# Output projection of the last batch as Strassen blocks, with a new order of all operations

## The chip, the cores and the metric

The kernel runs on one core of a Trainium2 chip. The core has five engines that run side by side and wait for one another through semaphores: TensorE (PE in the profile; its weight loads are PEld), VectorE (DVE), ScalarE (ACT), GpSimd (POOL) and SyncE (SP, which here only issues DMAs). The time is the device time of one execution in microseconds.

## The reference

Attention over 4 batches and 8 heads of 768 tokens, in which k and v are first mixed by an 8 x 8 matrix that five rounds of normalising have made nearly doubly stochastic; then a bilinear feed-forward layer on the result.

```python
def _moe_ref(x, w_a, w_b, w_out):      # x: 3072 x 512, one row for each token
    a = x @ w_a                        # 512 x 1536
    b = x @ w_b
    return (a * b @ w_out).astype(np.float32)   # 1536 x 512
```

The change touches the last product, `(a * b) @ w_out`, for the 768 tokens of the last batch. Below, h stands for `a * b`, and hT for h transposed, as the kernel keeps it.

## The kernel before

Each batch goes through attention (by pairs of heads), through the products with w_a and w_b, and through the product with w_out. Several batches are under way at once: attention of batch b+2 lies between the feed-forward work of batches b and b+1, and the loads run ahead of that.

**Feed-forward, batch 0** (`ab_plain`): four matmuls of 384 columns for each block of 128 features, then on ACT a copy of a and on DVE a product into hT.

**Feed-forward, batches 1 to 3** (`ab_strassen`, PE line L954): a and b by Strassen's method in Winograd's form. Both halves of the tokens and both halves of the features make up a 2 x 2 block problem, which takes 7 block products instead of 8. The features are cut into 6 groups g; in each group PE runs seven products p1 to p7, each a block of four matmuls of 384 columns. Two PSUM pairs take them, kA and kX. ACT copies the running sum of kA to SBUF three times (`snap`, L960: s1, u2, u3); DVE adds kX to these copies (`plus`, f<-f,ps: c11, c22, c12); four products make hT, of which one reads PSUM and runs on DVE (h21, hT<-a,ps, after an ACT cast, L990) and three read SBUF (hT<-f) and run on POOL or DVE. The fifth product of a group waits for c11, the third for c22, since they share kX. The sums of x that these products need are `x_sums` (tx), those of the weights `w_sums` (ws_a, ws_b, 128x768 each).

**Output** (`out_plain`, L1011): for each half t of the tokens and each chunk c of 128 columns, 12 matmuls of 512 columns add up over the 12 feature blocks in one PSUM bank; ten of them may run before the last group of h is done. Then a copy to SBUF on ACT or DVE (L317 and L319) and two stores from SP (L1031).

**The order.** Every piece of work is added to a `Plan` with the engines that may do it. `solve` doesn't choose: it reads the order of all pieces, and the engine of each, from the byte string `ORDER`, two digits of base 91 for each piece (its number times two, plus which of its engines). So ORDER fixes the queue of every engine. Engines take their queues in order; an instruction that waits holds up all that stand behind it on its engine. DMA loads are issued by POOL, and stand in its queue beside its arithmetic.

**Taking turns.** Pieces marked `port=("POOL", "DVE")` (sums with both inputs in SBUF, and hT<-f) must not run on POOL and DVE at the same time: `emit` makes the next one wait for the last one of the other engine.

```python
            if op.eng in op.port:
                for e, name in ported.items():
                    if e != op.eng:
                        tc.add_manual_dep(new[0], name, info, reason="one of them at the port")
                ported[op.eng] = new[-1].name
```

**Which output is used** is chosen near the end of the kernel function. Before, STRASSEN_OUT is empty, so all four batches use `out_plain`:

```python
        if b in STRASSEN_OUT:
            if wt_ok is None:
                wt_ok = o_sums(RB - 10.0)
            out_strassen(b, RB + 40.0, wt_ok)
        else:
            for t in range(2):
                for c in range(3):
                    out_plain(b, t, c, RB + 40.0)
```

Of the kernel before, what the change touches and what calls it, by code (L numbers as in the profile page):

```python
# [36 lines left out]
class Plan:  # L37
# [192 lines left out]

RATE = 365e3
ORDER = (
    b"$e1;%z###%#'#)#+#/#-#1#5$g$i#7#;$k$m#A$o#=$q$s#G#3$u$w#C#M$y%^${#I$}#9#S%`%#%%#Y%'#O#?%)%+"
    b"#`#E%-%/#U#f%1%~%3#[#K%5#l&$%7%9#b#r%;#Q%=#W%?#x%A#h%C&@#~%E#n#^%G&B%I$(%K#t%M#d$.%O%Q%S#j"
    b"$4#z%U&_$$#p%W$*&a%Y%b$0%f#v$:%d%[$6&&%h'&)#&g#|&(&H&j%n$&'A%j&K$,&*%p&2%m$<$2&L)'&,&D&O&4"
    b"&k&G%r&n&P'^%t&.$8&R$@%v&c$B$F&1&e%x&T%}'''z)%&}&V')&X&6$>'#&o&8'Y&:$H&q'`&Z$L']&<'b&s&^'="
    b"&?'h&u'?'C&w$N$D$R'+'j'd'.'v-b'E'g&y'/'x&|'G'|'1'J*($T$J(#$X'3**'5-n'7((*0($*,$Z$P('(**@$_"
    b"(,(6*.(.(0(<$a'9$V*B';*2(B*X*H(H*4-j(8'l$]*6'n'p*](>*<'r(N*Z-V't(D$c-R*L(T*a(:-_*_(Z(J-T*8"
    b"(@(a-Z(P+f-X(g*N(F+i*c(m(V*:(L(s+j-]*T(]+^*>-d(R+l'K,4(c+a*e'M(X,6,,(y(i'O(_,.-h*g'Q(o'S*i"
    b"*m(e'U(u,]'X)),X(k-a(2)/,T({,Z,_*k(q)5(4,W)+,a-));*q*o(w-+,c)A,i*s(},k)G+b-l*y*P*}+d)1,8-f"  # L240
    b"+x)-,;+#+z,e+n*R+p)M,g*D*V)S+r)7*F-p+t+)+%+v)3,0*J+|)Y,2+'+~+9,$)=,<++,F,>)C+;)9)`+-,H)I,@"
    b"+A,J)?)f,B+/,D)O+=)E)l+5,L,N)U--+?-/)K+E)[)r+C-1+I)Q)x)b+G-3)W)~+K+M.R)h)^+O+1.T,m)n)d+3,o"
    b",q,s+Q+7,u)j.Z-5+S)t.],w-7+Y/%,y._+U,{/')p/U)z/Q+W.a/W)v-%+[*u*$-'/S/-*w//)|.c-9,&,(-C*{-;"
    b".*-E/1,}.e*&-=-G/~-?.H-I-A,*-K,P/3.,-#-M/)../Y.V/+/[0$.0.J.X/C.M/9.4/E/5,R/^/;.N-O.q.g.s.6"
    b".21=/p.8.u/7.>.w/r.:1@/`.i.P.k.<.@1A/f/b.m.B-r1C/h.D.o/d.y0*/=.F0,/G-|/?0./I/A00/K/j0&/l1j"
    b"/n0(-t021l06-w0@-~0804-x1r.%0B1n1t.&1E1p-z/t1G1x/v2-1v1z/x.(1M1~0:1O1|0<2$2/2(0>1S2&1I1U2*"
    b"0D201W0F1K221`0H1Q1d241b260N1Y2:0P0T281[2<0Z0V2@1^2>2B0]0a2Q2V0R1i0g2D2F2X0m0X4L2L1g2_0c4N"
    b"2N2H0s0i2S2a4P0y2Z2J0_4H0o2e1#2]0e3C2g4R2c0k3E2u4J2i2k4T2T3K2q4{2s3M1)0u0q2m2x4w1/4}3Q2o0{"
    b"4V155#3S3G2z2{4y5%0w3U2}3I5'5K0}4X3^3'1%3c5M3O3`3)3#3W5)4]3-3%4_3d4Z3Y3/3>4g1+3+1'3[4i5+31"
    b"5G11333f5-59396D5O5;3;353?5Q1-3r17.{.}5I37135S3B0J5x3t5z4a/z3w3h/#4c195t5[3x5|5^5U3|5~0L/M"  # L250
    b"4e/|4k6$3~4m5W5f4o4$5v5/3j5h4&443m513z3n/O53465566576&485=4>5Y5?684:5A4(6I6(3p6N4<5`6F6P5j"
    b"4@5b6*6J4*4B5d4D6L5l5n6R6V4F6T8(6X4,8*6]6n6Z4.806_408,826c6a8.6o86426i6e6k888F846g8:8<6q7`"
    b"8B6,8D7b8H8>7d6.8@7h7f8J6s7j607l8#6u627n646{7p6w6}7t7r7%6y8$7z7v7'7|757#7x6:7)7+8&7;716<7-"
    b"787=737C7/7?7E6>798L7A7I8N8P7Z7K8T8R7M8V8l8X7U8Z7W7G8]8{7O8a7[7Q8n8c7S8q4q6@8e7^4s8p6B8_9G"
    b"5C8g9Q4u8i5p5E8}9I9#8s5r9L9)9%8u9S9M9'9=9V8w9O939W8y9Y9?9[9A9+9^9C9`9.9d9b9/959f:$9E9{979j"
    b":&999h91:(9l:,9p9;9n:.:*9|9r9v:29t:B:0:49x9~:H:8:6:J:L:E:>:P:N:::R:@:g:T:<:V:G;5:X;9;7:]:Z"
    b";;:i;=:c:_;S:e;?;A:a;C:l:m;E:q:o;I;G:s;U:u;O;K;Q:w;/:y;M:{;X;Y:};^;[;%;#;`;1;';+;b;-;x;f;)"
    b";d<,;4;h<@;j;n;{;p;l;r<T;t;};v<B<6<D<F<.<V<0<H;~<Y<2<Z<8<4<$<:<J<'<<<]<(<L<><N<P<*<R"
)
STRASSEN_OUT = ()  # L260
QDMA = lambda b, p: 4 * b + p >= 10
VDMA = lambda b, p: 4 * b + p >= 6
XDMA = lambda p: False
# [4 lines left out]
def kernel(  # L268
# [959 lines left out]
    for b in range(B):  # L1228
        if b in STRASSEN_OUT:
            if wt_ok is None:  # L1230
# [112 lines left out]
```

The softmax here doesn't subtract the row's maximum and nothing guards it: scores larger than these inputs give would overflow.

## Time and profile before

| | us |
|---|---|
| median of 7 runs | 245.35 (244.51 to 245.63) |
| the profiled execution | 244.51 |
| its span, first to last instruction | 242.7 |
| PE busy by stretch: 0 to 20, 20 to 40, 40 to 60 | 16.64, 18.69, 20.00 |
| PE busy 100 to 120, 180 to 200, 230 to 243 | 19.76, 20.00, 8.19 |
| DVE busy 100 to 120, 160 to 180, 180 to 200 | 17.93, 16.06, 8.36 |
| POOL busy 100 to 120, 180 to 200 | 13.09, 2.63 |
| granted TensorE clock, mean | 0.996 of full |

Busy time is read per engine and stretch; a PE that is busy all through may still run below its rate, since the ends of matmuls are modelled and overlap. A group's row names line, engine, operation, what is written and read, shapes, how many, then busy time, mean of one in ns, and the idle time before them with what ended it. In a timeline each row has start, duration, engine, line, operation and count, and in brackets the idle time before it.

The last products with w_a and w_b end at 226.8 us; from there on PE runs only output matmuls of batch 3, until 238.2.

### The profile page before, as it was taken

What the parts mean: (1) busy time and instruction counts of PE and PEld (TensorE: products, weight loads), DVE (VectorE), ACT (ScalarE), POOL (GpSimd) and SP (SyncE); (2) the same over time, 40 slices, a digit from 0 to 9 for tenths busy, and PEclk for the clock granted to TensorE, in tenths of its full rate; (3) what the DMA queues carried; (4) which work ended last, traced back from release to release, by engine and by line L of the source; (5) the groups of instructions that cost most, each with busy time, mean ns of one, the idle gap of its engine ahead of it and who ended that gap; (6) DMA issues with size and microseconds to landing.
All of it is one profiled execution on the core that took longest, in us unless ns stands there. A gap on an engine that the chain in (4) does not pass through costs nothing.

```text
span 242.7 us, 5334 instructions
## 1 busy us (share of the span) xinstructions
PE 232.6 (96%) x2125; PEld 130.7 (54%) x2125; DVE 154.3 (64%) x309; ACT 118.1 (49%) x177; POOL 101.9 (42%) x116
## 2 busy tenths in 40 slices
PE   8699989999999999999999999999999999999992
PEld 3367655656665445565554455556554455555440
DVE  6658748737574616699899346678873248874520
ACT  3268635764455452856664242665612066563110
POOL 8769899996610020039933020254120205433000
PEclk9999999999999999999999999999999999999998
DMA  5999999999997965509999787200008650000066
GB/s 69 170 188 116 201 174 194 201 208 195 193 206 150 132 171 130 120 1 120 141 162 185 148 197 167 58 0 4 0 0 122 140 125 5 3 0 0 0 132 130
DMA packets 54296, 28.27 MB, mean 116 GB/s; under 512 B 33536, under 2 KB 51200, under 8 KB 54272
## 3 DMA queue, kind: packets, MB, share of 16 engines
q0 software_dynamic: 26704, 14.16, 45.0%
q1 hardware_dynamic: 27568, 13.78, 29.4%
q8 instruction: 17, 0.28, 0.5%
q14 instruction: 7, 0.06, 0.1%
HBM read 30.29 MB, written 8.26 MB: 159 GB/s over the span
## 4 chain that ended last, share of the span: by engine, by line
PE 77%; DMA 12%; POOL 7%; issue 2%; ACT 1%; DVE 0%; ACTq 0%
PE ps L954 30%; PE ps L1011 26%; PE ps L860 10%; DMA v<-in_v_dram 6%; DMA qT<-q 4%; PE ps L694 3%; PE ps L572 2%; PE ps L679 2%; DMA w_a_sb<-in_moe_w_a_dram 2%; POOL k L440 1%; PE ps L638 1%; PE ps L556 1%; POOL q L428 1%; POOL v L440 1%; POOL s_all L523 1%
## 5 line engine op out<-in xcount | busy, mean ns | idle before, releaser
L1011 PE MATMUL ps<-w_out_sb,hT 128*128 128x512 bf16 x288 | 67.0, 379 | 0.0
L374 DVE TENSOR_TENSOR f<-f,ps 128x768 f32<-128x768 f32 x54 | 50.3, 950 | 15.8 <-ACT f L960 9.1
L374 POOL TENSOR_TENSOR hT<-f 128x384 bf16<-128x384 f32 x28 | 27.6, 1000 | 71.4 <-DVE f L374 71.3
L960 ACT COPY f<-ps 128x768 f32<-128x768 f32 x54 | 42.3, 801 | 29.4 <-PE ps L954 28.9
L1011 PEld LDWEIGHTS <-hT 128*128 128x128 bf16 x288 | 26.9, 98 | 29.5 <-ACT o L317 0.2
L684 ACT ACTIVATE eT<-ps 96x768 bf16<-96x768 f32 x32 | 25.2, 807 | 10.5 <-PE ps L679 10.2
L954 PE MATMUL ps<-tx,ws_a 128*128 128x384 bf16 x108 | 26.5, 327 | 0.5 <-ACT f L960 0.5
L374 DVE TENSOR_TENSOR hT<-a,ps 128x384 bf16<-128x384 bf16 x42 | 22.0, 548 | 7.6 <-ACT a L990 2.5
L954 PE MATMUL ps<-tx,ws_b 128*128 128x384 bf16 x108 | 26.4, 326 | 0.0
L317 ACT COPY o<-ps 128x512 f32<-128x512 f32 x15 | 8.8, 586 | 27.7 <-PE ps L1011 27.5
L705 DVE TENSOR_TENSOR xp<-ps,rec 96x512 bf16<-96x512 f32 x32 | 21.6, 683 | 0.7
L374 POOL TENSOR_TENSOR tx<-xT 128x768 bf16<-128x768 bf16 x3 | 4.9, 1635 | 37.0 <-DMA xT<-xp 37.0
L860 PE MATMUL ps<-xT,w_a_sb 128*128 128x384 bf16 x96 | 19.0, 327 | 0.7 <-DMA w_a_sb<-in_moe_w_a_dram 0.7
L860 PE MATMUL ps<-xT,w_b_sb 128*128 128x384 bf16 x96 | 19.1, 327 | 0.1
L954 PEld LDWEIGHTS <-ws_b 128*128 128x128 bf16 x144 | 14.1, 98 | 9.3
L954 PEld LDWEIGHTS <-ws_a 128*128 128x128 bf16 x144 | 12.7, 98 | 11.1 <-ACT f L960 2.0
L700 DVE RECIPROCAL rec<-ps 96x8 f32<-96x8 f32 x32 | 6.3, 200 | 18.4 <-PE ps L694 18.2
L317 ACT CAST kT<-ps 128x768 bf16<-128x768 f32 (+1 forms) x18 | 12.3, 696 | 11.5 <-PE ps L572 11.0
L954 PE MATMUL ps<-xT,w_a_sb 128*128 128x384 bf16 x72 | 17.6, 326 | 0.0
L954 PE MATMUL ps<-xT,w_b_sb 128*128 128x384 bf16 x72 | 17.6, 326 | 0.0
L990 ACT CAST a<-ps 128x384 bf16<-128x384 f32 x18 | 8.6, 479 | 15.7 <-PE ps L954 15.6
L374 DVE TENSOR_TENSOR hT<-f 128x384 bf16<-128x384 f32 x26 | 14.4, 555 | 2.3 <-POOL hT L374 1.2
(92 smaller groups left out, 322.2 us busy)
## 6 DMA issues: line engine op xcount, KB each, us to landing
out_dram<-o SPq DMA_DIRECT2D x48, 128.0 KB, 2.4
k<-in_k_dram POOLq DMA_DIRECT2D x16, 192.0 KB, 6.7
v<-in_v_dram POOLq DMA_DIRECT2D x16, 192.0 KB, 7.0
q<-in_q_dram POOLq DMA_DIRECT2D x20, 96.0 KB, 6.1
vd<-vm SPq DMA_DIRECT2D x10, 192.0 KB, 3.2
vs<-vd SPq DMA_DIRECT2D x10, 192.0 KB, 3.1
w_a_sb<-in_moe_w_a_dram POOLq DMA_DIRECT2D x4, 384.0 KB, 6.0
w_b_sb<-in_moe_w_b_dram POOLq DMA_DIRECT2D x4, 384.0 KB, 6.4
```

Of the source, the lines that this page charges most:

```text
L317: nc.scalar.copy(out=out, in_=in_)
L374: ENG[eng].tensor_tensor(out=out, in0=in0, in1=in1, op=op)
L440: nc.gpsimd.dma_start(out=buf((name, b, p)), in_=_ap(t, (b * H + 2 * p) * S * D, [[W, P], [S * D, 2], [1, W]]))
L684: nc.scalar.activation(out=buf(("eT", b, p, h))[:, :, 0:HB], in_=buf(("sc", b, p, h))[0:BLK, :, 0:HB], func=AF.Exp, scale=float(scale))
L694: nc.tensor.matmul(ops_[:, e, i * OW:(i + 1) * OW], lhsT=eT[:, e, i * BLK:i * BLK + P], rhs=vs[:, h * NBH + i, e * OW:(e + 1) * OW], start ...
L700: nc.vector.reciprocal(out=buf(("rec", b, p, h)), in_=_ap(buf(("op", b, p, h)), 0, [[1024, BLK], [512 + D, 2], [OW, NBH]]))
L705: nc.vector.tensor_tensor(out=_ap(xp, h * NBH * 2 * D, [[NB * 2 * D, BLK], [D, 2], [2 * D, NBH], [1, D]]), in0=_ap(ops_, 2, [[1024, BLK], ...
L860: nc.tensor.matmul(pf[:, u, 0:HW], lhsT=w_sb[:, kc, (m + u) * P:(m + u + 1) * P], rhs=buf(("xT", b))[:, kc, t * HW:(t + 1) * HW], start=(k ...
L954: nc.tensor.matmul(buf(key)[:, n, 0:HW], lhsT=lf(n, j), rhs=rf(j), start=start and j == 0, stop=j == 1, skip_group_check=not start)
L960: return add("ACT", 0.8, lambda: nc.scalar.copy(out=buf((name, b, g)), in_=buf(kA)[:, :, 0:HW]), [dep], get=[("f", (name, b, g))], rank=rk)
L990: e21 = add("ACT", 0.48, lambda: nc.scalar.copy(out=buf(("c21", b, g))[:, 0, :], in_=buf(kA)[:, 0, 0:HW]), [p4], get=[("a", ("c21", b, g)) ...
L1011: nc.tensor.matmul(po, lhsT=hT[:, t * 2 + m // G, m % G, c * P:(c + 1) * P], rhs=w_out_sb[:, m, :], start=(m == 0), stop=(m == KO - 1), sk ...
```

## The change

Two constants change. STRASSEN_OUT names batch 3, so that its output goes through `out_strassen` with the sums of w_out from `o_sums`; and ORDER is another string as a whole (1229 pieces instead of 1167), found by a longer search.

```diff
 ORDER = (
-    b"$e1;%z###%#'#)#+#/#-#1#5$g$i#7#;$k$m#A$o#=$q$s#G#3$u$w#C#M$y%^${#I$}#9#S%`%#%%#Y%'#O#?%)%+"
+    b"%z1;$e###%#'#)#+#/#-#1#5$g$i#7#;$k$m#A$o#=$q$s#G#3$u$w#C#M$y%^${#I$}#9#S%`%#%%#Y%'#O#?%)%+"
...
-STRASSEN_OUT = ()
+STRASSEN_OUT = (3,)
```

What ORDER now says, engine by engine: the loads keep their order, but the sums that stand among them on POOL are placed differently; PE, ACT and DVE have a new order from the first attention blocks on; 42 of the 54 products hT<-f of batches 1 to 3 are on POOL and 12 on DVE (28 and 26 before).

`o_sums` makes four blocks of 768 x 256 out of w_out (halves of its rows and of its columns), in eight pieces of 128x768 in bf16; all but one run on POOL. `out_strassen` makes four sums of h for each of the six groups, 24 pieces of 128x384 in bf16, in buffers that attention no longer needs:

```python
            todo = ((0, lambda g=g: (hb(1, 0, g), hb(1, 1, g)), ALU.add, h21 + h22, None),
                    (1, lambda g=g: (sb(0, g), hb(0, 0, g)), ALU.subtract, h11, 0),
                    (2, lambda g=g: (hb(0, 0, g), hb(1, 0, g)), ALU.subtract, h11 + h21, None),
                    (3, lambda g=g: (hb(0, 1, g), sb(1, g)), ALU.subtract, h12, 1))
```

Then, for each chunk c of 128 columns, seven products of six matmuls of 256 columns:

```python
            p1 = pe(kA, h(0, 0), wo(0, 0), False, True, hd(0, 0, late) + [p1], rk - 0.5, gs=late)
            s1 = snap("os1", p1)
...
            p2 = pe(kX, h(0, 1), wo(1, 0), False, True, hd(0, 1, late) + [p2], rk - 0.4, gs=late)
            c11 = plus("os1", kX, 0, 0, [s1, p2], [kX, ("os1", b, c)])
            p6 = pe(kA, s(1), wt(1), False, True, [s1] + sd(1) + td(1), rk, put=sput(1) + tput(1))
            u2 = snap("ou2", p6)
            p5 = pe(kY, s(0), wt(0), True, True, sd(0) + td(0), rk + 0.1, get=[("bank", kY)],
                    put=sput(0) + tput(0))
...
            p7 = pe(kA, s(2), wt(2), False, True, [u2] + sd(2) + td(2), rk, put=sput(2) + tput(2))
            u3 = snap("ou3", p7)
            p4 = pe(kZ, h(1, 1), wt(3), True, True, [p1, p2] + hd(1, 1) + td(3), rk + 0.6,
                    get=[("bank", kZ)], put=tput(3))
            c22 = plus("ou3", kY, 1, 1, [u3, p5], [("ou3", b, c)])
            c21 = plus("ou3", kZ, 1, 0, [u3, p4], [kZ, ("ou3", b, c), ("och", b, c)])
            p3 = pe(kY, s(3), wo(1, 1), False, True, [c22] + sd(3), rk, put=sput(3))
            c12 = plus("ou2", kY, 0, 1, [u2, p3], [kY, ("ou2", b, c), ("och", b, c)])
```

`snap` is an ACT copy of 128x256 from PSUM, `plus` a DVE add of 128x256. p1 and p2 run five of their six matmuls early, without the last feature block. Each half of the tokens is stored when both its column halves are there, by two stores; for the last chunk one of the two is issued by SP and the other by ACT:

```python
                    (nc.scalar if last and u else nc.sync).dma_start(
```

More of the change, by code (lines that the diff above doesn't have):

```diff
@@ L232 @@
 ORDER = (
-    b"$e1;%z###%#'#)#+#/#-#1#5$g$i#7#;$k$m#A$o#=$q$s#G#3$u$w#C#M$y%^${#I$}#9#S%`%#%%#Y%'#O#?%)%+"
+    b"%z1;$e###%#'#)#+#/#-#1#5$g$i#7#;$k$m#A$o#=$q$s#G#3$u$w#C#M$y%^${#I$}#9#S%`%#%%#Y%'#O#?%)%+"
     b"#`#E%-%/#U#f%1%~%3#[#K%5#l&$%7%9#b#r%;#Q%=#W%?#x%A#h%C&@#~%E#n#^%G&B%I$(%K#t%M#d$.%O%Q%S#j"
-    b"$4#z%U&_$$#p%W$*&a%Y%b$0%f#v$:%d%[$6&&%h'&)#&g#|&(&H&j%n$&'A%j&K$,&*%p&2%m$<$2&L)'&,&D&O&4"
-    b"&k&G%r&n&P'^%t&.$8&R$@%v&c$B$F&1&e%x&T%}'''z)%&}&V')&X&6$>'#&o&8'Y&:$H&q'`&Z$L']&<'b&s&^'="
@@ L237 @@
[L237 to L258, printed above, removed]
+    b"$4#z%U&_$$#p%W$*&a%Y%b$0%f#v$:%d%[$6&c%h'&)'&g#|&e&*&j%n$&'z&H&-$,&k%p&o&K$<$2&.$@&q&&&n&L"
+    b"&1)%&(&s&O&D'A&u%j&w$B$8&F&2'^%m'v$F&4%r'y&y)#'|%t&|&P'~$H$>%v&6&R($&8''&:&}(&$L&T'$'C')&V"
@@ new lines @@
+    b"'=$N$D$R&X'E%x&<'?'+-f%}((&>'.&Z'K(*&^'Y$T$J'`'M']*($X'c'G-j'h'J**'j$Z$P'/'d*0$_*@'g'1(,(6"
+    b"*B(.(0-b$a$V*,*H(2*.(5*L(<*2(8$]'O(B*X-V(H*D(>'Q-R*N(N'S(D$c*F-n*T(:*e*J(J+b(@*Z(T-T(P+d+f"
+    b"-_(Z(F*a*g(V-X(a+^+i-Z(L(g'U(]*]-]*m(m(R'X*P-a+`(c(s,0(X*R(y,2(i,4*V))(_+x,7(o*_-d(e*i+z*c"
+    b"(u'l*k(k-l'n({*4'p(q,,*o)+'3,.*6-h(w'5'r'7+n*<,8(}'u+p'9-p,T,;,<';,W--,>+j-/*8)/+l)-,@-1)1"
+    b")5*:,B,D);+9-3*>)A,X+;,Z)G*q)M+A-%)7)S,F-(,],H*s)3)Y,_+=-5*y,a+--7+?,J+C)=*u,c+/)9)`,L,s,N"
+    b"+5*w)C+E,u*{)I)?)f-)+G-+)O+r+Q+M)E)l+t+v,e)U-C.Z-E)K.V,g.]+S)r.X)Q+1)x._)[+Y*})W)~.a+3)b+U"
@@ new lines @@
+    b"+7.R)h)^+W.U-9.c+[)n/)-;+#)d.e/+-=+I-?)j+)-A/Y+K/[)t+%+O/^.g)p-G)z/Q.i+'/`-I-K/%,&/-,P/(.q"
+    b"*$)v-|/S//.s-M)|++/10&/b/C0(,i,R-~*&,k+|.%/~.*/E+~,$.&-O,m,w,o0*,(,q.4/30,/d,y0.0$,{/U/5.k"
+    b",}/W.,.m.(.u.o.6../9.w,*.8.0.y/f-r/;00/h.:/7/j-#1=/p06/l02/r/n-t.>.2-w08.<-x1?041A/G.@/I1C"
+    b"/=-z.B.H/?/A.D/K0:.J.F0<1E0>.L/t1G.N0@/v1I/x0B1M1K0D1O3C.P0F1e1Q3E0H1S0N3K1U0P0T3G3M1Y0Z1W"
+    b"0V3Q3I1`1[3S0]0a1b3O0R1^1f3U0X3W0g1j3^0c4L0m1l1i3Y3`0i4N1r3[0_0s4P4H1t0o1n4R0y0e221#3g4T1x"
+    b"240k1p4J4{1z2:3b1v4}3d0u1|0q2<1~4w262,2(0{4V2@282.2$2B4y2*1)2>0w2&2D1/0}4]4X2F202L2V1%4_2N"
@@ new lines @@
+    b"2H2R2X4Z4g2J155#4i2_5%2{2a1+2P5/5'5O2}1'2e112T5Q5G515)3'2g2Z5S171-3#3)2]5I2i133%2u5+3-2q2c"
+    b"2s3/3=3+2k315U19332w5x396D5t2m5z5-3;3?352o5|.{0J5K5v372y3|5M5~.}3A0L/M4*/#5W/z/O5[535^4,6$"
+    b"555Y3~574.4k4>4%/|406F4m6&4&4a424@4c5f4e6I4B3h6(5h4o4(4D6*6J3r6L4F5`3t5b5j5d3v593j5l5;3x5n"
+    b"443l3n3z6,6s6.5=3p466u5?6w5A486{6y4:8(6}767#8*607%624<64807'8,827+7)868.77717-88738F847/8:"
+    b"8<797;8B667=8D8H8>7?688@7C7A8J6:7E6N6<7G7Z6P7I6>6V<%7K6R6X7O7M<-6]6T7U7Q6_7W6Z7S6m6a6c<+7`"
+    b"6i7b7d6k6e<#7f7h6g7l7j7^8L7n7[8N8P6o7p8T8R7~7r8V7t8X6q7z8Z7|<'7v8]8q7x8$8a</8_8c8g9Q8{8i8m"
@@ new lines @@
+    b"4q5C8e8&5p8o5E9G4s8k5r<)6@9)4u<06B8}9+9#939T9.9%9/9V9=9'9W91:$9Y9?:&959B8s97:,9C8v:(:.9I8w"
+    b":*:29K9E;Y:C:49M:0;[8y;^:899:6;`9O:D;b:>:::@;d;x;f9;:<;h:G;5;j<>;9<:;7;n<=;l;=;;;z;t;p;?;v"
+    b";S;A;r;C<@9[;};E<_9`9^;I<[;G9b9d;U;O;K9f;Q9z9h;M9j<]:H;X9l<a:L:J<V9p9n<S:P:N9v9|9r:R9x:g:T"
+    b"9t:V<T:m:X:#<X:q:o<6:]:Z<3:u:c:s:i:_:w:e;/:y:a:{<c<4:}:l=/<8<e;#;%<g<G=W;+;1;';-=Y=1;)=5<C"
+    b"=[=3<i;4=7=^<D<k=E<J<H<y<L<m<Q<o=9<s<q<N<u=?<w<{=;<}=#===+=A=%=d=C='=G=h=f=-=I=K=S=j=M=)=`"
+    b"=l=b=n=O=p=U=r=t=|=v=Q=x=~=z"
```

## The prediction

> **What bounds the kernel now.** I read the page's busy table first, then the chain of waits, then the timeline of the end and of the start, and the groups for durations.
>
> ```profile
> PE 232.6 (96%) x2125; PEld 130.7 (54%) x2125; DVE 154.3 (64%) x309; ACT 118.1 (49%) x177; POOL 101.9 (42%) x116
> ...
> PE 77%; DMA 12%; POOL 7%; issue 2%; ACT 1%; DVE 0%; ACTq 0%
> ```
>
> TensorE is busy throughout and holds 77% of the chain that ended last; the DMA and POOL shares of that chain all lie before 40 us, apart from one transfer near 120 us. From 40 us on, time is won by taking work off TensorE, provided that it stays fed; before 40 us by earlier loads. Busy PE is modelled, so I take rates from runs of matmuls:
>
> ```profile
> 25.20 0.62 PE L660 MATMUL ps<-ident,vT 128*128 128x128 bf16 x8
> ...
> 216.47 0.49 PE L954 MATMUL ps<-xT,w_a_sb 128*128 128x384 bf16 x2
> ...
> 226.80 11.39 PE L1011 MATMUL ps<-w_out_sb,hT 128*128 128x512 bf16 x52
> ...
> 238.27 0.58 ACT L317 COPY o<-ps 128x512 f32<-128x512 f32 x1 [2.48 <-PE ps L1011]
> 238.88 1.10 SPq L1031 DMA_DIRECT2D out_dram<-o  x2
> ```
>
> The 52 matmuls of 512 columns take 11.39 us, the last of them 0.379 (its group's mean): 11.01/51 = 0.216 each. Two of 384 columns take 0.49, less a last one of 0.327: 0.163. Eight of 128 columns: (0.62-0.22)/7 = 0.057. The three lie on one line: 0.413 ns a column and some 4 ns. The reader sees also where the program ends: last matmul, a copy of 0.58, two stores issued one after the other, and 2.7 us until the span's end at 242.7.
>
> **The output projection of batch 3, PE.** Removed: 72 matmuls of 512 columns, 72 x 0.216 = 15.55 us. Added: 7 products x 3 token chunks x 6 = 126 of 256 columns. No row has 256 columns; the line gives 256 x 0.413 + 4 = 0.110, so 13.86 us: **1.7 us less**. [...] But here each of the x8 above has its own weights and still takes 57 ns. I go by the row[...].
>
> **Sums, copies and adds around it.** ORDER, read off per engine, puts 24 sums of h (17 on DVE, 7 on POOL), 8 of w_out (7 POOL, 1 DVE), 9 copies on ACT and 12 adds on DVE, in place of 6 output copies. It also gives POOL 42 of the 54 products hT<-f instead of 28, DVE 12 instead of 26.
>
> ```profile
> L374 POOL TENSOR_TENSOR hT<-f 128x384 bf16<-128x384 f32 x28 | 27.6, 1000 | 71.4 <-DVE f L374 71.3
> L374 POOL TENSOR_TENSOR tx<-xT 128x768 bf16<-128x768 bf16 x3 | 4.9, 1635 | 37.0 <-DMA xT<-xp 37.0
> L374 DVE TENSOR_TENSOR hT<-f 128x384 bf16<-128x384 f32 x26 | 14.4, 555 | 2.3 <-POOL hT L374 1.2
> L374 DVE TENSOR_TENSOR tx<-xT,tx 128x768 bf16<-128x768 bf16 x6 | 3.3, 543 | 2.0 <-POOL tx L374 1.9
> ```
>
> The w_out sums have w_out's 128x768 shape, so 1.635 on POOL: 11.4 us, put where batch 2's last groups run; POOL is busy 2.63 of the 17 us from 180 to 197. They are needed 30 us later: nothing. A sum of h is 128x384 bf16, a shape with no row. 384 f32 cost 555 on DVE and 768 bf16 543: between the 128x768 and 128x384 f32 rows (950, 555) an element costs 1.03 ns, leaving 160 fixed; so 160 + 384 x 0.50 = 0.35, bounds 0.30 and 0.555. On POOL: about 1.0.
>
> Do they fit beside TensorE? A group of 28 matmuls takes it 28 x 0.163 = 4.56 us. DVE per group: three adds of 0.95, hT<-a,ps 0.55, one hT<-f 0.555, three sums 0.35: 5.0 end to end, but two adds back to back read 1.82, so 0.08 less for each: 4.4. POOL: two hT<-f and one sum, 3.0. The code lets DVE and POOL work only in turn where both read SBUF twice, so POOL's 3.0, DVE's 0.48 + 3 x 0.27 and two handovers of 0.1 (a DVE add ends at 202.65, POOL starts at 202.74) must fit as well: 4.5 of 4.56. Both fit, barely. What waits behind a late sum on DVE is the next f<-f,ps, and PE's fifth product of a group behind that; walking one period through I find 0.2 us in hand there.
>
> **The end, walked.** T = 0 at the last group's first matmul. Before, this is 216.47, and the copy ends at 238.85: 22.38. Both versions have nine blocks of four 384-column matmuls left there, 5.87. After, with 0.65 per block or product (5 of 6 matmuls 0.55): the fourth product of this group ends at 6.4, its third at 7.6; by then five of six matmuls of the first products have filled in. ACT's cast and DVE's product let h21 be ready at 7.7, just as the matmuls that read it come. DVE's add of the third ends at 8.75; hT<-f 9.36; four sums in a row to 10.75. PE is at 10.9 before it needs them (p6 of chunk 0). POOL's sum and then DVE's last (in turn) are done at 12.25, p7 could go at 12.14: 0.2 lost. From there copies (0.37 on ACT, from 479 at 384 and 586 at 512) and adds (0.42, as the 128x256 rows from PSUM) lie beside other chunks, until the last: p7 of chunk 2, copy, two adds, then p3: 0.5 lost. Sum: 5.87 + 13.86 + 0.7 + 0.24 (drain and handover) + 0.42 = 21.1, **1.3 us less**. Then the stores: the last two issue on two queues instead of one after the other (0.47 and 0.59): **0.5 less**. Nothing here issues a DMA from ACT; bounds 0 and 0.6. Its older store is issued 0.5 us sooner, so it isn't in the way.
>
> **The start.** ORDER keeps the loads' order on POOL but moves what stands between them.
>
> ```profile
> 17.30 3.98 POOL L523 TENSOR_TENSOR s_all<-mask,p_col 128x1024 bf16<-128x1024 bf16 x2
> 21.22 0.80 POOL L457 DMA_DIRECT2D w_a_sb<-in_moe_w_a_dram  x1
> 22.01 0.75 POOL L457 DMA_DIRECT2D w_b_sb<-in_moe_w_b_dram  x1
> 22.77 2.02 POOL L523 TENSOR_TENSOR s_all<-mask,p_col 128x1024 bf16<-128x1024 bf16 x1
> ```
>
> One s_all, not two, now stands ahead of the w_a load: issued at 19.2 instead of 21.2. The page's slice there moves 116 GB/s against 170 to 208 around it, so the DMA engines have room and later loads come up to 1 us sooner. PE waited 0.74 for w_a at 30.98 and 0.50 for v at 39.91; that is what can be won. Against it: a weight sum of 1.65 moves ahead of that v load, issued 0.8 later. Loads there land 7 us after issue, one a microsecond: a backlog, so the issue isn't what counts. I take **-0.4**, bounds -1.2 and +0.8.
>
> **The stages between.** PE's, ACT's and DVE's orders are new from some 15 us on. POOL takes 14 products off DVE (7.8 us), which is 90% busy from 100 to 120. The waits view shows PE waiting for ACT there twice, 0.5 us together; a block of four matmuls misplaced costs 0.65. I take 0, bounds -1.5 and +2.
>
> **The sum.** 244.51 (the profiled execution) - 1.3 - 0.5 - 0.4 = 242.3. That execution was the fastest of the seven shown; from the median of 245.35 the same gives 243.15; I forecast **243.1**.
>
> **Rivals.** (a) *Slower: the turns.* [...] The trace agrees in that each takes turns here (hT<-f waits for POOL 1.2 us in all), and has 0.06 us spare per group by my sum. If a sum takes the 555 ns row, DVE's group is 5.0, 0.45 over PE's: five groups 2.2, five sums at the end 1.0, so 243.1 + 3.2 = 246.3. It decides from a sum of about 0.41 on. For it: three engines near full at once; against: the 543 of 768 bf16. (b) *No gain:* the new order loses in the middle what the end wins, 2.2 us, three or four misplaced blocks: 245.3. For it: both orders hang on a planner's durations; against: PE's waits there are few in the old one, and DVE gets relief. (c) *More:* that relief and the loads reach their bounds, -1.5 and -0.8 more: 240.9.
>
> **How the numbers follow.** Forecast 0.58 (241.8 to 244.6), (a) 0.18, (b) 0.10, (c) 0.14. No change means within 0.2% (0.5 us), what a measurement can tell. From the forecast's case nearly all is faster, with 0.02 same and 0.02 slower; (b) splits 0.02 faster, 0.03 same, 0.05 slower; (a) slower but for 0.01 same. Faster 0.70, same 0.06, slower 0.24. The range runs from (c) to (a): 241.0 to 246.4.
>
> **What would show it.** PE: 126 matmuls of 256 columns 0.11 apart[...]. DVE's sums of 128x384 bf16 at 0.35. From the last group's first matmul to the last add 21.1 us, with PE's only waits there at the seventh product of chunk 0 and before the last. Two last stores side by side. The second w_a load issued near 19.2, and v of batch 1 landing before 39.8. The forecast is wrong if DVE lags in batch 3, so that PE waits for f<-f,ps group after group, or if PE's stages from 40 to 197 us shift by over a microsecond.

## The result, and the profile after

| | before | after |
|---|---|---|
| median | 244.93 (64 runs) | 243.74 (27 runs) |
| ratio, 95% interval | | 0.9939 [0.9921, 0.9957] |
| profiled execution's span | 242.7 | 241.9 |

Faster by some 1.5 us by the ratio, 1.2 by the medians, where the forecast had 2.2 off its median of 245.35; the time itself lies inside the range, 0.6 above the forecast. The page's busy table and its chain of waits:

```profile
PE 230.9 (95%) x2178; PEld 136.3 (56%) x2178; DVE 155.8 (64%) x325; ACT 118.1 (49%) x180; POOL 133.0 (55%) x144
...
PE 84%; DMA 6%; POOL 5%; issue 2%; DVE 1%
```

TensorE still bounds. (Code lines are those of before plus 2.) The timeline of the end, where the forecast's largest term lies (start, duration, engine, line, operation, count, idle time before it):

```profile
217.38 0.49 PE L956 MATMUL ps<-xT,w_a_sb 128*128 128x384 bf16 x2
...
221.93 1.25 PE L1106 MATMUL ps<-w_out_sb,hT 128*128 128x256 bf16 x10
...
236.69 0.50 PE L1106 MATMUL ps<-w_out_sb,k 128*128 128x256 bf16 x3 [0.20 <-DVE s_all L376]
...
237.56 0.42 DVE L376 TENSOR_TENSOR o<-f,ps 128x256 f32<-128x256 f32 x1 [0.60 <-PE ps L1106]
238.00 0.47 SPq L1169 DMA_DIRECT2D out_dram<-o  x1
238.01 0.50 ACTq L1169 DMA_DIRECT2D out_dram<-o  x1
```

Ten matmuls of 256 columns take 1.25, less a last one of 0.27 for nine steps: 0.109 each. The last group's first matmul starts at 217.38 and the last add ends at 237.98: 20.60, where before it was 22.38. The two stores start side by side and the span ends 3.9 after the add, as long as before after its copy.

Did DVE and POOL keep up in batch 3? Busy time by stretch, one group each; after each engine's name its busy time and count, at the end the granted clock, the DMA share and GB/s:

```profile
203.60:208.20 4.60, 4.60 (x30) 2.74 (x29) 4.41 (x8) 2.78 (x4) 2.84 (x3) 1.00 0.00 0
208.20:212.80 4.60, 4.60 (x30) 2.79 (x29) 4.38 (x8) 2.78 (x4) 2.87 (x3) 1.00 0.00 0
212.80:217.40 4.60, 4.60 (x31) 2.78 (x30) 4.52 (x9) 2.78 (x4) 2.84 (x3) 1.00 0.01 4
```

The columns are PE, PEld, DVE, ACT, POOL. DVE is busy 4.4 to 4.5 of 4.6 us and TensorE never waits for it here. A sum of h takes DVE 0.35:

```profile
208.05 0.35 DVE L376 TENSOR_TENSOR k<-hT,k 128x384 bf16<-128x384 bf16 x1
```

The loss is earlier. Lines of the timeline from the start and from 71 to 83 us:

```profile
19.50 0.80 POOL L459 DMA_DIRECT2D w_a_sb<-in_moe_w_a_dram  x1
...
31.11 0.81 PE L862 MATMUL ps<-xT,w_a_sb 128*128 128x384 bf16 x4 [1.60 <-DMA w_a_sb<-in_moe_w_a_dram]
...
72.26 0.54 SPq L649 DMA_DIRECT2D vd<-vm  x1
80.34 0.31 SPq L653 DMA_DIRECT2D vs<-vd  x1
...
80.39 0.96 DVE L321 CAST vm<-ps 128x768 bf16<-128x768 f32 x1 [2.84 <-PE ps L574]
...
81.41 0.34 PE L681 MATMUL ps<-qT,kT 64*128 64x96 bf16 x8 [1.03 <-DVE vm L321]
82.33 0.34 PE L681 MATMUL ps<-qT,kT 64*128 64x96 bf16 x8 [0.58 <-DVE hT L376]
```

The w_a load that was issued at 21.22 before goes at 19.50, but lands at 26.43 (26.33 before). At 31.11 PE has waited 1.60 for the next w_a load, where before it waited 0.74; the wait of 0.50 for v, landed at 39.45 instead of 39.77, is gone. At 80 to 82 a chain ends that begins with a transfer: the store of vm to DRAM, issued at 72.26, lands at 80.27; only then may DVE write that vm buffer (there are two), and PE waits for DVE twice, 1.6 together. The releaser named in DVE's row, PE, had long been done with what this cast reads (L640, ended at 77.38); the row at 80.34, which waits for the same landing, gives it away. Before, PE had no wait there. So my reading after the result was: 1.8 won at the end, some 0.3 to 0.9 lost before it.

Below I give medians of all executions beside the ratios, because the ratios leave out those over 1.5% above a kernel's fastest, which were 8 of 22 for a repeat of the changed kernel.

### The profile page after: what moved, and what is told of

The parts are those of the page before. It is cut to its first block, busy times and chain, and to the rows that moved or that the text cites. A ratio compares the mean times of both kernels' runs of the same rounds, so it can differ in the third digit from the quotient of the medians.

```text
span 241.9 us, 5514 instructions
## 1 busy us (share of the span) xinstructions
PE 230.9 (95%) x2178; PEld 136.3 (56%) x2178; DVE 155.8 (64%) x325; ACT 118.1 (49%) x180; POOL 133.0 (55%) x144
## 4 chain that ended last, share of the span: by engine, by line
PE 84%; DMA 6%; POOL 5%; issue 2%; DVE 1%
PE ps L956 34%; PE ps L1013 20%; PE ps L862 13%; PE ps L1106 5%; PE ps L696 3%; DMA v<-in_v_dram 3%; PE ps L574 3%; PE ps L681 3%; DMA w_a_sb<-in_moe_w_a_dram 2%; PE ps L640 2%; POOL k L442 1%; PE ps L558 1%; POOL q L430 1%; POOL v L442 1%; POOL w_b_sb L459 1%
## 5 line engine op out<-in xcount | busy, mean ns | idle before, releaser
L376 POOL TENSOR_TENSOR hT<-f 128x384 bf16<-128x384 f32 x42 | 41.2, 1003 | 63.6 <-DVE f L376 47.4
L376 DVE TENSOR_TENSOR f<-f,ps 128x768 f32<-128x768 f32 x54 | 49.8, 951 | 14.6 <-PE ps L956 9.8
L1013 PE MATMUL ps<-w_out_sb,hT 128*128 128x512 bf16 x216 | 50.5, 379 | 0.0
L1013 PEld LDWEIGHTS <-hT 128*128 128x128 bf16 x216 | 19.8, 98 | 21.3
L956 PEld LDWEIGHTS <-ws_a 128*128 128x128 bf16 x144 | 13.3, 98 | 9.7 <-DVE f L376 0.9
L319 ACT COPY o<-ps 128x512 f32<-128x512 f32 x12 | 7.0, 585 | 19.1 <-PE ps L1013 18.9
L956 PEld LDWEIGHTS <-w_b_sb 128*128 128x128 bf16 x108 | 10.6, 98 | 7.0
L696 PEld LDWEIGHTS <-eT 96*128 96x128 bf16 x256 | 11.7, 98 | 4.7
```

Of the source, the lines that this page charges most:

```text
L319: nc.scalar.copy(out=out, in_=in_)
L376: ENG[eng].tensor_tensor(out=out, in0=in0, in1=in1, op=op)
L696: nc.tensor.matmul(ops_[:, e, i * OW:(i + 1) * OW], lhsT=eT[:, e, i * BLK:i * BLK + P], rhs=vs[:, h * NBH + i, e * OW:(e + 1) * OW], start ...
L956: nc.tensor.matmul(buf(key)[:, n, 0:HW], lhsT=lf(n, j), rhs=rf(j), start=start and j == 0, stop=j == 1, skip_group_check=not start)
L1013: nc.tensor.matmul(po, lhsT=hT[:, t * 2 + m // G, m % G, c * P:(c + 1) * P], rhs=w_out_sb[:, m, :], start=(m == 0), stop=(m == KO - 1), sk ...
```

## The experiments

The strings of ORDER are long; where an edit changes them, it is given in short, by what it moves.

### The halves of the change

**The new order with the plain output.** The pieces of batches 0 to 2 and of the start from the new order, then the old order for batch 3:

```diff
-ORDER = (old)
+ORDER = (new, as far as batch 3's stage; then old)
 STRASSEN_OUT = ()
```

> The new order of batches 0 to 2 and of the start, with the plain output for batch 3 and the old order there. Theory (the new order costs, the Strassen output wins): the profile of the changed kernel shows TensorE 0.6 to 0.9 us behind the old one from 30 us on and 1.8 us won from the last group on, so this kernel has the loss alone: ratio to before 1.002 to 1.004, 0.5 to 0.9 us slower. Rival (the longer search is what won, the Strassen output little): faster by 1 us or more, ratio 0.996 or lower.

Measured: 1.0013 [0.9989, 1.0036], 245.31 us against 244.81. The rival, that the order before the last stage brought the gain, is out: 0.996 lies outside. Whether that order costs 0.9 us or nothing, the interval leaves open.

**The old order with the Strassen output.** The other half; the w_out sums on DVE, since POOL's old order has other work there:

```diff
-ORDER = (new)
+ORDER = (old, as far as batch 3's stage, 8 w_out sums on DVE; then new)
 STRASSEN_OUT = (3,)
```

> The old order up to batch 3's stage, then the new order with the Strassen output; the eight w_out sums are all on DVE, inside batch 2's last groups. Theory (all of the gain comes from the end): 1.8 us won at the end and nothing lost before it, ratio to before 0.991 to 0.993, so some 0.7 us better than the changed kernel (0.994). Rival (the new order is what won): ratio 0.998 to 1.001. A third possibility: the 8 x 0.55 us on DVE push its adds late, and PE waits for f<-f,ps near the end of batch 2 by up to 1 us: 0.995 to 0.997 with such waits in the trace.

Measured: 0.9913 [0.9881, 0.9945], 242.53 us: 2.1 us less than before. With the new order in front of both, the last stage is worth 0.9939/1.0013 = 0.9926, 1.8 us. The two agree: **all of the gain is the last stage's**, the Strassen output with the order that belongs to it, and the eight DVE sums cost nothing that shows.

### The start

**One block moved.** In PE's order the first block with w_b, whose load had landed at 22.9, goes ahead of the block that waits for w_a's third load.

```diff
-PE: ... a(m=4, u=0), x, a(m=4, u=1), b(m=0, u=0), xT, b(m=0, u=1) ...
+PE: ... b(m=0, u=0), a(m=4, u=0), x, b(m=0, u=1), a(m=4, u=1), xT ...
```

> The changed kernel, with two pieces of PE's order exchanged: the first block with w_b (landed at 22.9 us) goes ahead of the block that reads the third load of w_a (landed at 31.0). Theory (the misplaced block is what costs at the start): PE's wait of 1.60 us for w_a at 31.1 us shrinks to under 0.3 us or goes, and TensorE stays 0.7 to 0.9 us ahead of the changed kernel: ratio to before 0.990 to 0.991. Rival (the loads of batch 1 bound the start anyway, so that the wait only moves): the ratio stays at 0.994, and new PE waits for DMA of 1 us or more stand between 33 and 45 us.

Measured: 0.9882 [0.9833, 0.9930], from few runs: 242.89 is the median of six. The timeline shows both theories at work:

```profile
31.08 0.81 PE L862 MATMUL ps<-xT,w_a_sb 128*128 128x384 bf16 x4 [0.22 <-DMA w_a_sb<-in_moe_w_a_dram]
...
37.82 0.82 PE L862 MATMUL ps<-xT,w_a_sb 128*128 128x384 bf16 x4 [0.68 <-DVE xp L707]
39.00 0.53 PE L574 MATMUL ps<-s_all,k 128*64 128x128 bf16 x12 [0.36 <-DMA k<-in_k_dram]
```

The wait fell from 1.60 to 0.22; 1.04 of the 1.38 came back as waits for xp and for k of batch 1, which landed at 38.9. So most of it only moved in this execution. One profile says little here: six kernels that share the new start without this edit show this wait at anything from under 0.25 to 1.71. The intervals of this kernel and of the changed one overlap, and the times don't tell more.

**The term of my forecast alone.** In the kernel before, one s_all sum goes behind the second w_a load (from 30 us on some PSUM buffers are others, too):

```diff
-POOL: s_all, s_all, w_a(c=2), w_b(c=2), s_all
+POOL: s_all, w_a(c=2), s_all, w_b(c=2), s_all
```

> The kernel before, with one s_all sum of 2.0 us on POOL moved from ahead of the second w_a load to behind it, as the changed kernel has it; nothing else of the order changes (from 30 us on some PSUM buffers are others). My forecast's term for the start: the load issues at 19.2, later loads land up to 1 us sooner, 0.4 us faster: ratio 0.998. Theory from the trace of the changed kernel (issued at 19.5 it landed at 26.4, where the one issued at 21.2 landed at 26.3: a backlog, so the issue doesn't count): the load lands at 26.0 to 26.6 as before, ratio 0.999 to 1.001.

Measured: 1.0041 [1.0015, 1.0067], 245.76 us: **slower by 1 us**, which neither theory had. The load landed at 25.24, 1.1 sooner than before, which the second theory had excluded. Its timeline, and its busy time by stretch:

```profile
23.63 0.37 PE L556 MATMUL ps<-ident,q 64*64 64x64 bf16 x11
25.57 0.21 PE L556 MATMUL ps<-ident,q 64*64 64x64 bf16 x1 [1.56 <-issue]
```

```profile
26.00:28.00 2.00, 2.00 (x49) 1.53 (x46) 1.10 (x3) 1.75 (x4) 1.98 (x3) 0.81 0.99 142
28.00:30.00 2.00, 2.00 (x22) 1.23 (x21) 0.96 (x3) 0.81 (x1) 1.99 (x2) 0.50 1.25 190
30.00:32.00 2.00, 2.00 (x27) 1.30 (x26) 0.89 (x2) 0.47 (x1) 2.00 (x4) 0.84 1.20 179
```

TensorE stops after the eleventh of twelve equal matmuls, for 1.56 us, and nothing that the trace records releases it ("issue"). Then the granted clock, the third figure from the end of a row, falls to 0.50 for 3.4 us. What was TensorE short of? The page lists a DMA queue named "instruction" with 17 packets and 0.28 MB, 16 KB each; TensorE has 2125 matmuls and 2125 weight loads, 250 to a packet, so I take these packets to be its program: an estimate, since the trace does not say whose they are. The DMA view of a stretch shows whether it holds one (packets, MB, share of the engines); here 23.0 to 24.1 us of this kernel, and 21.4 to 22.6 of the kernel before:

```profile
q8 instruction: 1, 0.02, 5.1%
```

```profile
q8 instruction: 1, 0.02, 5.0%
```

The packet of this stretch starts at 21.46 in the kernel before and at 23.12 here; it ends at 24.01, and TensorE goes on 1.56 later. That distance comes back: in all seven profiles of this study in which TensorE stops like this near 24 to 26 us, it goes on 1.3 to 1.6 us after the end of the packet. Two more things point to the program. The packet ended at 22.71 or later in these seven and at 22.50 or earlier in the seven profiles without a stop. And TensorE stops each time after 704 or 705 of its recorded instructions, which is after the eleventh of twelve equal matmuls in the old order and after the fifth in the new: a fixed place in the program. In the kernel before the DMA engines had a lull around it: 42 GB/s from 22 to 24 us, where this kernel moves 152. **The lull that I wanted to fill is the one in which this packet came through.**

**The same kernel again:**

> A second execution of before_wa_early, for one look. Theory (the late packet of instructions goes with the earlier load, not with chance): the packet in the stretch from 20 to 25 us starts at 22.5 us or later and PE stands still for over 0.3 us at 23 to 26 us with nothing in the trace that releases it. Rival (chance): it starts near 21.5 us, without such a stall.

Measured: the packet starts at 23.81, TensorE stops for 1.84, and the clock is at half for 6.8 us from 25.1 on, which is before TensorE goes on; 247.19 us.

```profile
26.22 0.26 PE L556 MATMUL ps<-ident,q 64*64 64x64 bf16 x1 [1.84 <-issue]
...
24.00:26.00 2.00, 0.37 (x14) 0.26 (x11) 1.15 (x4) 0.00 (x0) 1.30 (x2) 0.77 1.10 152
26.00:28.00 2.00, 1.78 (x28) 1.51 (x29) 0.05 (x1) 1.48 (x3) 0.82 (x2) 0.50 1.00 152
28.00:30.00 2.00, 2.00 (x32) 1.39 (x29) 1.16 (x3) 0.83 (x3) 2.00 (x2) 0.50 1.00 154
30.00:32.00 2.00, 2.00 (x22) 1.12 (x21) 0.96 (x2) 0.58 (x1) 1.99 (x3) 0.52 1.16 172
```

The clocks of all timed executions say more. Half a clock for 3.4 us lowers the mean over 243 us to 0.993, so I part them at 0.994 (the others are at full clock, or nearly):

| kernel | under 0.994 | mean us of these | mean us of the others |
|---|---|---|---|
| before, beside before_wa_early | 2 of 34 | 247.0 | 244.6 |
| before_wa_early | 16 of 22 | 246.2 | 244.6 |
| before, beside new_start_plain_end | 1 of 48 | 245.7 | 244.8 |
| new_start_plain_end | 9 of 22 | 245.8 | 244.8 |
| after_again (below) | 9 of 22 | 245.3 | 242.6 |
| after_wa_late (below) | 3 of 22 | 246.2 | 244.0 |

16 of 22 against 2 of 34 is no chance, and the whole loss of before_wa_early sits in these 16: the other 6 take what the kernel before takes. The new order, with the plain output, likewise shows no cost at full clock. Beside loads that fill the DMA engines (a share of 1.21 and 1.26 from 22 to 24 us, where the kernel before has 0.64) TensorE stood for 1.56 and 1.84 us here.

**The edit the other way round**, in the changed kernel, beside the changed kernel itself on one chip:

```diff
-POOL: s_all, w_a(c=2), s_all, w_b(c=2), s_all
+POOL: s_all, s_all, w_a(c=2), w_b(c=2), s_all
```

> The changed kernel itself, on the same chip as the three beside it, so that they can be set against it. Expected: ratio 0.992 to 0.996.

> The changed kernel, with two s_all sums instead of one ahead of the second w_a load, as the kernel before has it (it is the edit of before_wa_early the other way round; some PSUM and SBUF buffers are others from there on). Theory (the lull in the loads near 22 us lets TensorE's next packet of instructions through; where loads fill it, the packet comes up to 1.7 us later and PE stands still): the packet starts near 21.5 us, PE has no unexplained stall at 23 to 26 us, ratio 0.4% better than the changed kernel on this chip if it is as in the kernel before; nearer 0.1% if the changed kernel's own packets come late only now and then (the profiles of its start show stalls of 0.3 to 0.5 us in four of seven). Rival (the packet's time is chance, and the load's earlier issue is worth 0.4 us): 0.1 to 0.2% worse than the changed kernel.

Measured: the changed kernel 0.9905 [0.9882, 0.9929], median 243.41; with the late load 0.9961 [0.9941, 0.9981], median 244.26. The packet came at 20.73, without a stall at 23 to 26, as expected; but the kernel is 0.85 us slower by the medians, 1.4 by the ratios. The means of all 22 executions of each differ by 0.6, with a 95% interval from -0.3 to 1.5; those at full clock, the last column of the table, by 1.4 (0.8 to 2.1). **In the new order the early load wins something at full clock**, as the rival and the forecast had it in sign, and gives some of it back, since 9 of 22 executions lost clock with it and 3 without: what is left over is not clear of noise. The new order's own packet starts at 21.1 to 22.9 us in the profiles and PE loses 0 to 0.5 there. What the early load wins I could not trace: in the profile of the late one PE waits 1.26 for w_a and 0.84 for a POOL weight sum near 39 us, and the buffers differ as well.

### From 40 to 197 us

**The weight sums behind the loads.** In the changed kernel, four POOL sums stand ahead of the second w_out load; they go behind it and behind the first loads of batch 2:

```diff
-POOL: w_out(0), ws, ws, ws, ws, w_out(1), w_out(2), k, v, q, k, v, q ...
+POOL: w_out(0), w_out(1), w_out(2), k, v, q, ws, ws, k, v, ws, q, ws ...
```

> The changed kernel, with four weight sums of 1.7 us each on POOL moved from ahead of the second and third w_out load and the first loads of batch 2 to behind them (the second w_out load then issues near 44.8 us, not 51.1). Theory (late loads make a gate at 80 to 89 us: the store of vm to DRAM queues with them, takes 8 us, DVE waits for its buffer, PE for DVE 1.6 us): these waits at 80 to 82 us go, batch 2's last load lands some 5 us sooner, 0.5 to 1.2 us better than the changed kernel: ratio to before 0.989 to 0.992. Rival (the loads are bound by the DMA engines or by the freeing of buffers, not by when POOL comes to them): loads land as before, ratio 0.993 to 0.995. Third: the sums come too late for the first Strassen products, PE waits for POOL near 75 to 80 us: 0.996 or more.

Measured: 0.9886 [0.9842, 0.9930] from six runs, median 241.28, the lowest of all kernels here. The loads, and the stores of vm from SP:

```profile
43.01 2.25 POOL L467 DMA_DIRECT2D w_out_sb<-in_moe_w_out_dram  x3
...
58.92 0.53 SPq L649 DMA_DIRECT2D vd<-vm  x1
67.77 0.31 SPq L653 DMA_DIRECT2D vs<-vd  x1
68.13 0.53 SPq L649 DMA_DIRECT2D vd<-vm  x1
...
75.97 0.31 SPq L653 DMA_DIRECT2D vs<-vd  x1
```

All three w_out loads go at 43.0; the store that was issued at 72.26 goes at 68.13 and still takes 7.8, so it lands at 75.9, not at 80.3. PE has no wait left from 76 to 92 us, and batch 2's last load lands at 78.9 (82.4). The path of that stall is shown; that the place of the sums decides it is not. Of seven profiles with the sums ahead of the loads, three (new_start_plain_end, after_wa_late, dve_hsums_twice) have no wait at 80 us either. What goes with the wait is the landing of that store: 80.1 to 80.7 us in the four with it, 78.4 or earlier in the six without, of which the three with the sums behind have 75.4 to 77.3. The price of the edit is 0.5% between two intervals that overlap, and this profile also waited 0.81 for w_a at the start instead of 1.60, which the edit doesn't touch.

**With the first start edit too:**

> Both edits of order in the changed kernel: the first block with w_b ahead of the one that waits for w_a's third load, and the four POOL weight sums behind the loads. If the start's gain is absorbed at the gate at 80 to 89 us as long as that is set by transfers, the two together are worth more than the sum of each alone: ratio to before 0.985 to 0.988. If they add up or only one counts: 0.988 to 0.991. If neither counts beyond the start's changes from run to run: 0.993 to 0.995.

Measured: 0.9911 [0.9877, 0.9945], median 242.28. The stall at 80 us is gone here as well. The two edits are not worth more than their sum, and not visibly more than one of them.

**With the late load:**

> The edit of after_wa_late and that of wsums_behind_loads together, as a version to beat both kernels. If both count: ratio to before 0.984 to 0.988. If only the loads count: 0.988 to 0.991. If the first wins nothing and the second was luck of six runs: 0.992 or more.

Measured: 0.9938 [0.9911, 0.9964], median 243.05; beside after_wa_late on the same chip 1.2 us less by the medians, 0.6 by the ratios. Again PE has no wait at 80 us; but neither has the profile of after_wa_late, so what the 1.2 us are stays open. What the late load costs here can't be told: no kernel with the early load and the sums behind ran on this chip. No version is shown to beat the changed kernel beyond the intervals; wsums_behind_loads is the one to measure longer.

### The end

**Both last stores from SP:**

```diff
-                    (nc.scalar if last and u else nc.sync).dma_start(
+                    nc.sync.dma_start(
```

> The changed kernel, with the two last stores both issued by SP, one after the other, instead of one by SP and one by ACT. My forecast's term: the second issue queue is worth 0.5 us, so this one is slower than the changed kernel by 0.5: ratio to before 0.996, and 4.4 us from the last add's end to the span's end. Theory from the trace (the store issued by ACT landed 2.84 us after its issue, those of SP after 2.2 to 2.4, so the earlier issue is given back): within 0.2 us of the changed kernel, ratio 0.993 to 0.995, and 3.9 to 4.1 us from the last add to the span's end.

Measured: 0.9945 [0.9916, 0.9973], which can't separate 0.5 us from none. The profile can:

```profile
236.87 1.11 SPq L1169 DMA_DIRECT2D out_dram<-s_all  x2
237.43 0.42 DVE L376 TENSOR_TENSOR o<-f,ps 128x256 f32<-128x256 f32 x1 [0.59 <-PE ps L1106]
238.08 1.18 SPq L1169 DMA_DIRECT2D out_dram<-o  x2
```

The add ends at 237.85, SP is held by the older pair until 237.98, and the last store, issued at 238.66, lands at 241.03. From the add's end to the span's end it is 4.15, against 3.9 with two queues: the second queue is worth **0.25**, between the two theories.

**DVE's sums of h made twice:**

```diff
-                op.fn = lambda ...: tt(op.eng, sb(j, g), src()[0], src()[1], alu)
+                op.fn = lambda ...: [tt(op.eng, sb(j, g), src()[0], src()[1], alu)
+                                     for _ in range(2 if op.eng == "DVE" else 1)]
```

> The changed kernel, with each of the 17 sums of h that DVE makes made twice (the output stays the same). In batch 3's groups DVE is busy 4.4 to 4.5 us of the 4.6 that a group takes, with three sums in most groups; a second of two sums in a row takes 0.28. My forecast's rival (a), taken as a law for DVE's room: three more at 0.28 make a group 5.25, 0.65 over PE's, in 4 or 5 groups 2.6 to 3.3, and five sums more in a row at the end 1.4: 4.0 to 4.7 us slower than the changed kernel, ratio to before 1.010 to 1.013, with PE waiting for DVE (f<-f,ps) group after group from 204 us on. Rival (there is more room than the busy time says, because queued work slides until the end): under 2 us, ratio under 1.002, and PE's waits only after 224 us.

Measured: 1.0159 [1.0113, 1.0204], 2.2% or 5.4 us over the changed kernel, 4.5 by the medians; the spans of the two profiles differ by 3.9. PE's waits from 200 us on (engine, line waited for, total, times, longest):

```profile
PE ps L1106 <- DVE v L376: 1.4, 2, 1.0
PE ps L956 <- DVE f L376: 1.4, 3, 0.6
PE ps L1106 <- DVE s_all L376: 0.2, 1, 0.2
```

Both kinds of wait are there, f<-f,ps in the groups and the sums at the end. They add up to 3.0; the rest the list doesn't name. The end cost 1.6, near the 1.4 of the law; the groups cost 1.4 instead of 2.6 to 3.3, in three groups from 216 us on, not from 204: queued work first used up some room. Rival (a) had the right kind of cost, and batch 3 has little room on DVE.

## Why the prediction was right, point by point

- **Rate of 256 columns.** Forecast 0.110 by the line through three rows, measured 0.109. The busy tables count as many weight loads as matmuls (x2125 of both before, x2178 after), and with that 128 columns took 57 ns, 256 took 109, 384 took 163 and 512 took 216: the line, 0.413 ns a column and 4 ns, meets all four within 1 ns.
- **The end, -1.3:** -1.78 in the profile. The wait at the seventh product of chunk 0 (0.2) didn't come, and the last one was 0.2, not 0.5: together the 0.5 by which the walk was off.
- **The stores, -0.5: the term that was mis-sized.** Measured 0 against before. The mechanism is there: the second issue comes 0.01 after the first, not 0.51. But two stores started together land later (2.57 and 2.84 us after their issue; one after the other 2.24 and 2.38), which gives back 0.46. Against the same kernel with one queue it is 0.25, since there SP's older pair stands in the way, which I had excluded. The two errors at the end cancel: -1.8 forecast for both, 1.8 to 2.1 measured. That this sum came out is luck.
- **The start, -0.4: the step whose argument failed.** I read the slow slice of DMA near 22 us as room. In the kernel before, the packet that I take for TensorE's program also came in it (21.46 to 22.42), and the move that I priced at -0.4 costs 1.0 there. In the changed kernel, undoing it costs 1.4 at full clock and 0.6, not clear of noise, over all: right in sign, but for a reason that I can't show. Of what PE was to win, the 0.50 for v went, but the 0.74 for w_a became 1.60 in the changed kernel's profile, since the new order asks for w_a's third load ahead of a block that was ready (0.22 with that block first). That was in ORDER, and I had costed only POOL's part of it.
- **The stages between, 0:** within its bounds. A stall at 80 us is new, 0.4 to 1.8 in four of the seven profiles with this order there. Start and middle together, forecast -0.4, came to +0.3 [-0.3, +0.9] by new_start_plain_end, and what loss there is sits in the executions that lost clock, a term that the forecast did not have. The 0.7 between are what the forecast was short by.
- **Rivals.** (a) did not come, because the sum of h cost 0.35, below its turning point of 0.41; doubling it shows that more would have cost time. That DVE and POOL wait for each other (1.2 us for hT<-f before) shows only the order that the kernel sets: `emit` makes them take turns, and no run here leaves that out, so what they would do side by side was not shown. (b), the gain lost in the middle, happened in small. (c) did not.

## What to carry to other kernels

Take a change apart into halves that each run: here the last stage carried all the gain and the new order before it none that shows. A stretch in which the DMA engines idle isn't free room until it is known what passes through it (42 GB/s from 22 to 24 us in the kernel before; with 152 there the kernel took 1.0 us longer). And an earlier issue bought nothing by itself in the changed kernel (issued 1.7 sooner, the w_a load landed at 26.43 instead of 26.33): follow each load to the instruction that first waits for it, in the new order of that engine.

## What the hardware showed that I had not expected

- TensorE stood still for 1.56 and 1.84 us in before_wa_early and its repeat, both times after the eleventh of the same twelve matmuls, where a packet of 16 KB on the "instruction" queue came 1.7 and 2.4 us later than in the kernel before. That it ran out of program is my reading; the trace names nothing that it waited for.
- These two pauses cost twice: with them the granted clock fell to 0.50 for 3.4 and 6.8 us. Length alone does not decide: pauses of 1.60 (the changed kernel, at 31 us) and 1.71 (both_stores_sp) left the clock at 1.00 (the rows below are the changed kernel's, the clock third from the end), and after_again lost it for 3.4 us after waits of 1.21 and 0.58 at 80 us. What decides, no run here shows.

```profile
30.00:32.00 2.00, 0.89 (x12) 0.66 (x13) 0.00 (x0) 0.45 (x1) 2.00 (x2) 1.00 1.13 171
32.00:34.00 2.00, 2.00 (x22) 1.24 (x19) 1.21 (x3) 0.80 (x1) 1.99 (x3) 1.00 1.17 174
```

- In the changed kernel's profile the store of vm to DRAM (192 KB) took 8.0 to 10.4 us when it was issued between 52 and 73 us, beside the loads (151 to 202 GB/s in all from 52 to 76 us), and 2.2 to 4.6 from 80.7 us on.
